# A two-product attention-MLP kernel: the first product from scaled f16 pairs instead of float32r, its straddling tiles as two 64-column halves

## The chip, the cores and the metric

The kernel runs on one core of one Trainium2 chip. The metric is device time in microseconds (us) of one execution. The names of the engines are those of the profile: PE is TensorE (PEld its weight loads), DVE is VectorE, ACT is ScalarE, POOL is GpSimd, SP is SyncE, which issues the DMAs.

## The reference

Eight batches of eight heads, 576 positions of 64 numbers. Thirty-two "pack" queries p attend to k and v; the result serves as keys and values for q. The attention output, as rows of 512 numbers, goes through an MLP of width 1024 with a softmax gate and a layer norm:

```python
p_packed = sm_attn(p, k, v)
x = sm_attn(q, p_packed, p_packed)      # rows of 8 heads x 64 = 512
h = x @ w_in                            # 4608 x 1024
e = np.exp(h - h.max(-1))
solu = h * e / (e.sum(-1) + 1e-9)
ln = (solu - solu.mean()) / np.sqrt(solu.var() + 1e-6) * g_ln
out = ln @ w_out                        # 4608 x 512
```

w_in and w_out come as 64-bit floats, which the kernel reads as two 32-bit words each; it builds f32 values of w_in and a high and a low f16 part of w_out from them. The other inputs are f32.

## The kernel before, in words

The work of a batch b has three parts. `pack(b)` transposes k (kT, L350), takes the scores of p (L368) in two PSUM banks of the pool ps_a, their exponentials (L381), transposes these (L397), multiplies with v (L407), scales the result to pp (L411), transposes it on PE (L413) and copies it to ppT on DVE (L415). `unpack(b)` transposes q (L428), takes the scores of q against ppT (16 small matmuls, L467), transposes them on DVE (L439), does the softmax (maximum L443, subtraction on POOL L444, exponential on ACT L446, sum L448, reciprocal, product on POOL L451), and computes z = ppT . w_in (L483), so that the first product can be written h = a2 . z with the softmax weights a2 as left side. Both are split into a high and a low part: z into zh (a rounding cast on ACT, L485) and zl (a subtraction on DVE, L500), a2 after a transpose (L505) into a2h (ACT, L507) and a2l (DVE, L508).

The rows of the output are cut in 36 tiles of 128. For each, `mlp_in` sums in the bank pair h (pool ps_h, two buffers) three products, a2h.zh, a2h.zl and a2l.zh, for two head groups r and two column halves n: 12 matmuls 128x512 in float32r (L521). 576 is four and a half tiles, so every second tile border straddles two batches: four such tiles, each with rows of an even batch b and of b+1. There the tiles a2h and a2l have 64 zero columns of padding, and 24 full matmuls are summed. Then come the row maximum nm (DVE, L523), a bound of two small operations (L525, L526), its reciprocal s_row (L528), the exponential e with bias nm (ACT, L531), and u = e.s_row.h (DVE, L534). `mlp_norm` subtracts the mean (POOL L542) into an f16 pair yhl (ACT L544, DVE L545), which a transposing DMA on SP's queue turns into yT (L547); the squares and a row factor c_row go over ACT and POOL. `mlp_out` makes 24 f16 matmuls 128x512 (L564) in a bank of ps_o, DVE scales them to o_sb (L566), and SP stores (L571).

What sets the order: the program is written tile by tile, with tables (`FIRST_BATCH`, `LATER`, `LOADS`, `PACK0` and so on) that say how many steps of pack and unpack are taken ahead of, in and behind each tile, and with priorities. From batch 1 on PE's order is as written, by the tables; the other engines, and PE in batch 0, are ordered by a scheduler that simulates the program. pack runs two batches ahead of the tiles, unpack one. At the start, batch 0, w_in, w_out and the first pack are prepared (`high_part`, `add_low_part`, `prepare_w_out`), and PE runs filler matmuls (`keep_busy`).

## Time and profile before

| | us |
|---|---|
| median of 3 runs | 472.3 |
| lowest and highest run | 471.37 and 472.42 |
| span of the profiled execution | 468.9 |
| PE busy | 430.2 (92%) |
| DVE busy | 354.2 (76%) |
| ACT busy | 232.4 (50%) |
| POOL busy | 148.0 (32%) |

The runs are 3.4 us above the span in the median, which is what lies around the profiled part. A line of the profile's groups names the kernel line, the engine, the operation and its tile names, the number of instructions, then busy time, mean time of one in ns, and the engine's idle time before them with what ended it. The chain of waits is the work that ended last, followed back from the end; each of its pieces has a start, a length and a line. A row by stretch of time gives the length, the busy time of PE, PEld, DVE, ACT and POOL, the granted clock of PE, the share of the DMA engines and GB/s.

### The profile page before, as it was taken

Reading aid. Unit: us, or ns where it says so; the run is one execution under the profiler, and the core shown is the slowest. Engines: PE = TensorE matmul, PEld = TensorE weight load, DVE = VectorE, ACT = ScalarE, POOL = GpSimd, SP = SyncE. Lnnn points to the kernel's source line nnn. Section 1 sums busy time; section 2 is a strip of 40 time slices with the busy share of each in tenths; the row PEclk is TensorE's granted clock in tenths of the full one; section 3 lists DMA queues with packets and bytes.
Section 4 is the critical chain, followed back from the end, with each engine's and each line's share of the span. In section 5 each row is a group of like instructions: output and inputs, shape, how many; then the busy total and the mean of one; then the engine's idle time right before and its main releaser. Section 6 shows DMA issues by size and latency. Waiting matters only on the chain.

```text
span 468.9 us, 8271 instructions
## 1 busy us (share of the span) xinstructions
PE 430.2 (92%) x3116; PEld 234.7 (50%) x3116; DVE 354.2 (76%) x648; ACT 232.4 (50%) x404; POOL 148.0 (32%) x244
## 2 busy tenths in 40 slices
PE   9697795859979999999899998999999999999995
PEld 7472244633434555446544554566445555575552
DVE  3568989778768887988489979975898688655551
ACT  3577848654343653565244562653356536433430
POOL 3424556935103211421044123311342142111220
PEclk9979759988998999999999999999999999999999
DMA  9999999999569969965989588339035333526342
GB/s 265 336 268 286 152 207 124 135 193 155 110 138 185 169 127 181 191 142 95 204 111 135 109 177 154 89 69 214 23 68 113 69 69 83 119 67 134 70 101 78
DMA packets 237880, 67.00 MB, mean 143 GB/s; under 512 B 208912, under 2 KB 231440, under 8 KB 237328
## 3 DMA queue, kind: packets, MB, share of 16 engines
q1 hardware_dynamic: 237840, 66.48, 74.3%
q8 instruction: 24, 0.39, 0.4%
q14 instruction: 16, 0.13, 0.1%
HBM read 37.23 MB, written 9.44 MB: 100 GB/s over the span
## 4 chain that ended last, share of the span: by engine, by line
PE 58%; DVE 18%; DMA 10%; POOL 5%; issue 4%; SPq 2%; ACT 2%; DVEq 0%; ACTq 0%; POOLq 0%
PE po L564 30%; PE h L521 17%; DMA yT<-yhl 4%; DMA zh<-in_moe_w_in_dram 3%; PE pa L483 3%; PE pa L407 2%; PE pa L368 2%; DMA v_sb<-in_v_dram 2%; PE pa L397 2%; DVE yhl L545 2%; DVE nm L523 2%; DVE kT L350 2%; DVE u L534 1%; DMA p2raw<-in_p_dram 1%; PE pa L467 1%
## 5 line engine op out<-in xcount | busy, mean ns | idle before, releaser
L564 PE MATMUL po<-wch,yT 128*128 128x512 f16 x576 | 178.6, 380 | 4.5 <-DMA yT<-yhl 4.5
L564 PEld LDWEIGHTS <-yT 128*128 128x128 f16 x864 | 81.0, 98 | 116.5 <-issue 17.5
L564 PE MATMUL po<-wcl,yT 128*128 128x512 f16 x288 | 108.8, 379 | 0.0
L531 ACT ACTIVATE e<-h,nm 128x1024 f32<-128x1024 f32 x36 | 40.0, 1112 | 69.5 <-DVE nm L523 69.5
L521 PE MATMUL h<-zh,a2h 128*128 128x512 f32 x160 | 69.9, 437 | 1.7 <-DVE u L534 1.7
L544 ACT ACTIVATE yhl<-u,negmu 128x1024 f16<-128x1024 f32 x36 | 41.4, 1149 | 53.1 <-POOL negmu L542 51.2
L521 PE MATMUL h<-zl,a2h 128*128 128x512 f32 x160 | 64.2, 401 | 0.6 <-POOL zl L493 0.6
L521 PE MATMUL h<-zh,a2l 128*128 128x512 f32 x160 | 64.7, 404 | 0.0
L545 DVE SCALAR_TENSOR_TENSOR yhl<-u,negmu,yhl 128x1024 f16<-128x1024 f32 x36 | 48.5, 1346 | 15.5 <-ACT yhl L544 15.5
L523 DVE TENSOR_REDUCE nm<-h 128x1 f32<-128x1024 f32 x36 | 43.9, 1219 | 20.6 <-PE h L521 20.5
L534 DVE SCALAR_TENSOR_TENSOR u<-e,s_row,h 128x1024 f32<-128x1024 f32 x36 | 45.8, 1271 | 7.1 <-ACT e L531 5.0
L551 POOL TENSOR_SCALAR s_eps<-se,s_row 128x1 f32<-128x1 f32 x36 | 10.8, 301 | 110.9 <-ACT e L531 56.0
L554 POOL TENSOR_SCALAR c_row<-sq,s_eps 128x1 f32<-128x1 f32 x36 | 18.8, 521 | 78.9 <-ACT e L549 78.9
L549 ACT ACTIVATE e<-u,negmu 128x1024 f32<-128x1024 f32 x36 | 40.9, 1136 | 3.4 <-POOL negmu L542 3.4
L566 DVE SCALAR_TENSOR_TENSOR o_sb<-po,c_row,inv 128x512 f32<-128x512 f32 x36 | 26.7, 743 | 20.9 <-PE po L564 20.8
L521 PEld LDWEIGHTS h<-zh,a2h 128*128 128x128 f32 x160 | 31.2, 195 | 17.4 <-issue 8.2
L521 PEld LDWEIGHTS h<-zh,a2l 128*128 128x128 f32 x160 | 30.9, 193 | 8.7 <-DVE a2l L508 1.2
L521 PEld LDWEIGHTS h<-zl,a2h 128*128 128x128 f32 x160 | 31.0, 194 | 7.1 <-POOL zl L493 0.9
L485 ACT CAST zh<-pa 128x512 fp32r<-128x512 f32 x28 | 15.1, 583 | 23.3 <-PE pa L483 23.3
L444 POOL TENSOR_TENSOR s<-s,mx 128x576 f32<-128x576 f32 x14 | 16.9, 1229 | 30.2 <-DVE mx L443 30.1
L381 ACT ACTIVATE e<-pa,nmx 128x288 f32<-128x288 f32 x28 | 13.8, 499 | 21.6 <-DVE nmx L373 21.6
L221 POOL TENSOR_TENSOR u<-u 128x1024 fp32r<-128x1024 f32 (+1 forms) x5 | 12.9, 2573 | 28.3 <-ACT u L220 18.1
(138 smaller groups left out, 608.5 us busy)
## 6 DMA issues: line engine op xcount, KB each, us to landing
out_dram<-o_sb SPq DMA_DIRECT2D x36, 256.0 KB, 2.3
v_sb<-in_v_dram SPq DMA_DIRECT2D x16, 512.0 KB, 6.0
raw<-in_k_dram SPq DMA_DIRECT2D x28, 288.0 KB, 6.3
raw<-in_q_dram SPq DMA_DIRECT2D x96, 72.0 KB, 2.6
zh<-in_moe_w_in_dram SPq DMA_DIRECT2D x2, 1024.0 KB, 7.0
zl<-in_moe_w_in_dram SPq DMA_DIRECT2D x2, 1024.0 KB, 8.6
raw<-in_q_dram SPq DMA_DIRECT2D x4, 512.0 KB, 9.3
raw<-in_moe_w_out_dram SPq DMA_DIRECT2D x2, 1024.0 KB, 5.9
```

What stands on the lines that cost most here:

```text
L444: eng.tensor_tensor(out=s2[r], in0=s2[r], in1=mx.unsqueeze(2).broadcast_to([P, NB, J]), op=ALU.subtract)
L485: nc.scalar.copy(z_h[:, r, cols], pz)
L521: nc.tensor.matmul(h[:, 512 * n:512 * n + 512], lhsT=lhsT, rhs=z[:, r, 512 * n:512 * n + 512], start=t == 0, stop=t == len(terms) - 1)
L523: nc.vector.tensor_reduce(out=nm, in_=h, axis=AX.X, op=ALU.max, negate=True)
L531: nc.scalar.activation(e, h, AF.Exp, bias=nm, accum_out=se)
L534: nc.vector.scalar_tensor_tensor(out=u, in0=e, scalar=s_row, in1=h, op0=ALU.mult, op1=ALU.mult, accum_out=su)
L544: nc.scalar.activation(yhl[:, 0], u, AF.Identity, bias=negmu)
L545: nc.vector.scalar_tensor_tensor(out=yhl[:, 1], in0=u, scalar=negmu, in1=yhl[:, 0], op0=ALU.add, op1=ALU.subtract)
L549: nc.scalar.activation(e, u, AF.Square, bias=negmu, accum_out=sq)
L554: nc.gpsimd.tensor_scalar(out=c_row, in0=sq, scalar1=1.0 / DF, scalar2=s_eps, op0=ALU.mult, op1=ALU.add)
L564: nc.tensor.matmul(po, lhsT=yT[:, a, c], rhs=w[:, c], start=c == 0 and t == 0, stop=c == NFC - 1 and t == 2)
L566: nc.vector.scalar_tensor_tensor(out=o_sb, in0=po, scalar=c_row, in1=inv, op0=ALU.mult, op1=ALU.mult)
```

## The change

The four operands zh, zl, a2h and a2l become f16, each scaled by a power of two so that it fits; the straddling tile becomes 12 pairs of matmuls with 64 columns each, one half of a pair for each batch, into PSUM partitions 0 to 63 and 64 to 127. The zero padding and the four POOL operations that wrote it are gone.

The scale comes from a bound: at the start, eight f32 matmuls of ones with the absolute high words of w_in (L212) and a maximum give w_bound; in each batch a peak of |pp| (DVE, L425) and a 128x1 matmul that sums it (PE, L426, into a spare column of the bank that holds pp's transpose) give a power of two in three small DVE operations (L436 to L438) and three on POOL (L439 to L441). The factors stand in the tile unit. zh is an activation with that factor, zl a scalar_tensor_tensor. In each row tile the exponential gets a bias of its own (L551, one more small DVE operation between nm and the exponential). In a straddling tile POOL copies unit from the two batches (L536).

In the changed kernel the lines are shifted: L540 is L521, L585 is L564, L502 is L483, L486 is L467, L421 is L413, L423 is L415, L542 is L523, L544, L545 and L547 are L525, L526 and L528, L555 is L534, L510 is L500, L517 is L508, L566 is L545, L587 is L566.

```diff
+        if chunk < G:
+            for i in range(2):
+                nc.tensor.matmul(w_sums[0], lhsT=ones_f, rhs=bits.bitcast(F32)[:, 512 * i:512 * i + 512], start=chunk + i == 0, stop=chunk == G - 1 and i == 1)
+            if chunk == G - 1:
+                nc.vector.tensor_reduce(out=w_bound, in_=w_sums[0], axis=AX.X, op=ALU.max)
...
-        a2h.append(par.tile([P, 2, S + LEFT], F32R, name=f'a2h{par_i}'))
-        a2l.append(par.tile([P, 2, S + LEFT], F32R, name=f'a2l{par_i}'))
-        pad = slice(S, S + LEFT) if par_i == 0 else slice(0, LEFT)
-        for t in (a2h[-1], a2l[-1]):
-            nc.gpsimd.tensor_scalar(out=t[:, :, pad], in0=ones_f.rearrange('p (r x) -> p r x', r=2), scalar1=0.0, scalar2=None, op0=ALU.mult)
+        a2h.append(par.tile([P, 2, S], F16, name=f'a2h{par_i}'))
+        a2l.append(par.tile([P, 2, S], F16, name=f'a2l{par_i}'))
...
-        packed[b] = ppT
+        peak = small.tile([P, 1], F32, name='peak')
+        nc.vector.tensor_reduce(out=peak, in_=pp.rearrange('p r d -> p (r d)'), axis=AX.X, op=ALU.max, apply_absolute_value=True)
+        nc.tensor.matmul(ppt[:, P:P + 1], lhsT=ones_f, rhs=peak, start=True, stop=True)
+        packed[b] = (ppT, ppt)
...
+        nc.vector.tensor_scalar(out=power, in0=ppt[:, P:P + 1], scalar1=w_bound, scalar2=2.0 ** (-40), op0=ALU.mult, op1=ALU.max)
+        nc.vector.tensor_scalar(out=power.bitcast(I32), in0=power.bitcast(I32), scalar1=2139095040, scalar2=None, op0=ALU.bitwise_and)
+        nc.vector.tensor_scalar(out=unit[:, 0:1].bitcast(I32), in0=power.bitcast(I32), scalar1=-1, scalar2=254 + Z_TOP << 23, op0=ALU.mult, op1=ALU.add)
...
+                nc.scalar.activation(z_h[:, r, cols], pz, AF.Copy, scale=unit[:, 0:1])
...
+                    nc.vector.scalar_tensor_tensor(out=z_l[:, r, cols], in0=pz, scalar=unit[:, 0:1], in1=z_h[:, r, cols], op0=ALU.mult, op1=ALU.subtract)
...
-        for i, c in parts:
-            cols = slice(c, c + P)
+        m = P // len(parts)
+        groups = []
+        for x, (i, c) in enumerate(parts):
+            rows, cols = (slice(m * x, m * x + m), slice(c, c + m))
...
+            for t, side_by_side in enumerate(zip(*groups)):
+                for rows, lhsT, z, r in side_by_side:
+                    nc.tensor.matmul(h[rows, 512 * n:512 * n + 512], lhsT=lhsT, rhs=z[:, r, 512 * n:512 * n + 512], start=t == 0, stop=t == last)
...
-        nc.scalar.activation(e, h, AF.Exp, bias=nm, accum_out=se)
+        bias = small.tile([P, 1], F32, name='bias')
+        nc.vector.tensor_scalar_mul(bias, nm, unit[:, 1:2])
+        nc.scalar.activation(e, h, AF.Exp, bias=bias, scale=unit[:, 1:2], accum_out=se)
```

Three places in the order of the instructions matter below. The first is PE behind the transpose of pp in pack 6 (at 320 us of the profile before); pa is the bank of the transpose, po the output product. Before:

```order
L564 MATMUL po<-wch,yT 128x512
L413 MATMUL pa<-ident,pp 128x128
L564 LDWEIGHTS yT
L564 MATMUL po<-wch,yT 128x512
L564 MATMUL po<-wcl,yT 128x512
```

The same place after; qT and ppT are the operands of the q scores:

```order
L585 MATMUL po<-wch,yT 128x512
L421 MATMUL pa<-ident,pp 128x128
L486 MATMUL pa<-qT,ppT 32x288
L426 MATMUL pa<-peak,ones_f 128x1
L585 LDWEIGHTS yT
L585 MATMUL po<-wch,yT 128x512
```

One of the 16 q scores and the peak matmul moved between the transpose and the 12 output matmuls that followed it; the other 15 scores stay behind these. The same stands at packs 3 to 7.

The second is PE in the straddling tile of batches 4 and 5; a2h_182 and a2h_186 are the parities of the two batches. Before:

```order
L521 MATMUL h<-zh,a2h_182 128x512
L521 MATMUL h<-zl,a2h_182 128x512
L521 MATMUL h<-zh,a2l_183 128x512
L521 MATMUL h<-zh,a2h_186 128x512
L521 MATMUL h<-zl,a2h_186 128x512
L521 MATMUL h<-zh,a2l_187 128x512
```

After, a2h_183 and a2h_185 are the two batches:

```order
L540 LDWEIGHTS a2h_183
L540 MATMUL h<-zh,a2h_183 64x512
L540 LDWEIGHTS a2h_185
L540 MATMUL h<-zh,a2h_185 64x512
L540 LDWEIGHTS a2h_183
L540 MATMUL h<-zl,a2h_183 64x512
L540 LDWEIGHTS a2h_185
L540 MATMUL h<-zl,a2h_185 64x512
```

The two batches take turns, matmul by matmul, each with 64 columns and a weight load of its own.

The third is DVE around the second tile of batch 3 (at 254 us before); a2l, yhl, mx (a maximum of pack scores) and nmx belong to other tiles than nm. Before:

```order
L545 SCALAR_TENSOR_TENSOR yhl<-u,negmu,yhl 128x1024
L508 TENSOR_TENSOR a2l_183<-s_2927,a2h_182 128x576
L523 TENSOR_REDUCE nm<-h 128x1
L371 TENSOR_REDUCE mx_2667<-pa 128x1 x2
L525 TENSOR_SCALAR bound<-nm 128x1
L373 TENSOR_REDUCE nmx<-mx_2667 128x1
L526 TENSOR_SCALAR bound<-nm,bound 128x1
L528 RECIPROCAL s_row<-bound 128x1
L534 SCALAR_TENSOR_TENSOR u,su<-e,s_row,h 128x1024
```

After:

```order
L542 TENSOR_REDUCE nm<-h 128x1
L566 SCALAR_TENSOR_TENSOR yhl<-u,negmu,yhl 128x1024
L379 TENSOR_REDUCE mx_2767<-pa 128x1 x2
L544 TENSOR_SCALAR bound<-nm,unit 128x1
L517 TENSOR_TENSOR a2l_184<-s_3031,a2h_183 128x576
L551 TENSOR_SCALAR bias<-nm,unit 128x1
L381 TENSOR_REDUCE nmx<-mx_2767 128x1
L545 TENSOR_SCALAR bound<-nm,bound 128x1
L547 RECIPROCAL s_row<-bound 128x1
L555 SCALAR_TENSOR_TENSOR u,su<-e,s_row,h 128x1024
```

yhl and one a2l moved from ahead of nm to between nm and the new bias.

More of the change, by code (lines that the diff above doesn't have):

```diff
@@ L257, in packed_attention_solu_kernel @@
     nc.scalar.activation(warm, ones_f[:, :1], AF.Exp)
+    w_bound = const.tile([P, 1], F32, name='w_bound')
     neg_half = const.tile([P, 1], F32, name='neg_half')
@@ L505, in unpack @@
             nc.vector.transpose(out=a2T, in_=a2[r].rearrange('p a j -> p (a j)'))
[L506 removed]
+            hi, lo = (a2h[b % 2][:, r], a2l[b % 2][:, r])
             nc.scalar.copy(hi, a2T)
[L508 removed]
+            (nc.vector if b else EN(nc, A2L_BY[r])).tensor_tensor(out=lo, in0=a2T, in1=hi, op=ALU.subtract)
             yield
```

65 lines of the change are left out of this document (33 added, 32 removed).

## The prediction

> **What bounds the kernel now.** I read the page first: the span and the chain that ended last.
>
> ```profile
> span 468.9 us, 8271 instructions
> PE 58%; DVE 18%; DMA 10%; POOL 5%; issue 4%; SPq 2%; ACT 2%; DVEq 0%; ACTq 0%; POOLq 0%
> PE po L564 30%; PE h L521 17%; DMA yT<-yhl 4%; DMA zh<-in_moe_w_in_dram 3%; PE pa L483 3%; PE pa L407 2%; PE pa L368 2%; DMA v_sb<-in_v_dram 2%; PE pa L397 2%; DVE yhl L545 2%; DVE nm L523 2%; DVE kT L350 2%; DVE u L534 1%; DMA p2raw<-in_p_dram 1%; PE pa L467 1%
> ```
>
> PE is 58% of the chain, not all of it. So a PE saving counts only where PE ends last. The chain of waits in order of time gives the places.
>
> ```profile
> 144.48 3.49 PE h L521 x12
> 180.77 5.34 DMA v_sb<-in_v_dram
> 227.38 6.81 DMA yT<-yhl
> 280.52 7.02 DMA yT<-yhl
> 323.33 2.06 PE h L521 x9
> 326.04 3.64 PE h L521 x15
> 371.72 2.60 PE po L564 x12
> 402.91 2.74 PE h L521 x12
> 405.66 5.20 PE po L564 x24
> 410.85 8.18 PE h L521 x36
> 445.29 2.74 PE h L521 x12
> ```
>
> From 144.48 to 445.29 the chain holds 22 full tiles of first product (x12). I count 21: one, at 270, lies between a stretch on DVE and one on DMA. Two straddling tiles stand on it too: 24 instructions at 323.33 and 326.04, and 24 of the 36 at 410.85. The straddling tile at 226 ends in a wait for a DMA (227.38). The one before 126 belongs to the startup. The busy times by stretch tell where DVE is the bound:
>
> ```profile
> 186.00:203.00 17.00, 16.20 (x97) 8.22 (x96) 16.13 (x33) 8.79 (x15) 6.55 (x9) 1.00 1.19 179
> 237.00:268.00 31.00, 31.00 (x188) 15.45 (x186) 29.95 (x56) 15.86 (x28) 11.07 (x17) 1.00 0.78 115
> 288.00:329.00 41.00, 41.00 (x308) 23.28 (x307) 31.70 (x65) 20.76 (x37) 10.09 (x23) 1.00 0.51 116
> ```
>
> The columns are PE, PEld, DVE, ACT, POOL, clock. In 186 to 203 DVE works 16.13 of 17 us, in 237 to 268 29.95 of 31, and the chain runs on it; in 288 to 329 it has 9 us to spare and the chain is PE's.
>
> **The change, part by part.**
>
> *The matmul's type.* At 402.91 twelve matmuls take 2.74 us, 228 ns each. The f16 ones behind them (24 in 5.20) take 217 ns. If f16 brings the first product to the same rate, an ordinary tile saves 12 x 11 = 0.14 us; 21 tiles, 2.9 us. The low end is no saving, if the 11 ns belong to the accumulation and not to the type.
>
> *The straddling tile.* Before: 24 x 228 ns = 5.47 us. After: 24 half-width matmuls, two of which may run side by side: 12 x 217 = 2.60, so -2.87. That two 64-column halves share the array is shown by another pair of rows, both f32 with 128 columns streamed: 16 halves take as long as 8 full ones, whose row stands second.
>
> ```profile
> 13.62 1.09 PE L125 MATMUL h<-ident,raw 128*64 128x128 f32 x16
> 215.45 0.95 PE pa L397 x8
> ```
>
> I take -2.87; the other end is 24 x 217 = 5.21, -0.26. The difference is 2.6 us a tile. On the chain: 2 x 2.87 = 5.7.
>
> The page "TensorE: Matmul & The Clock Gate" of the Trainium skill, Part 3, says that a weight load overlaps matmuls in flight only where the row group differs. Two column halves have the same row group, so by that rule the halves need not overlap and the saving would be -0.26. The rows above are f32 without separate weight loads, so no run here shows it; the case is a rival below.
>
> *The straddling tile at 226.* Its next PE work waits for a transposing DMA that stands on SP's queue behind q and v loads:
>
> ```profile
> 217.59 6.23 SPq L85 DMA_DIRECT2D raw<-in_q_dram  x9
> 227.38 3.47 SPq L547 DMA_TRANSPOSE yT<-yhl  x1
> 232.40 0.39 PE L521 MATMUL h<-zh,a2l 128*128 128x512 f32 x1
> 234.23 0.39 PE L564 MATMUL po<-wch,yT 128*128 128x512 f16 x1 [1.44 <-DMA yT<-yhl]
> ```
>
> The order on SP is the same after the change here. So 2.87 us off PE only lengthens the wait of 1.44. Counted at nothing.
>
> *The peak matmul and a score ahead of it.* In the new order PE takes one q score matmul, which needs the copy of ppT, directly behind the transpose of pp. Before, twelve output matmuls stood there:
>
> ```profile
> 320.46 0.27 PE L413 MATMUL pa<-ident,pp 128*128 128x128 f32 x1
> 320.57 0.38 PE L564 MATMUL po<-wch,yT 128*128 128x512 f16 x1
> 320.77 0.29 DVE L415 COPY ppT<-pa 128x128 f32<-128x128 f32 x1 [0.90 <-PE pa L413]
> 325.32 0.72 PE L467 MATMUL pa<-qT,ppT 64*32 64x288 f32 x16
> ```
>
> PE would idle from 320.57 until the copy has ended (321.06), then run the lone score and the peak matmul before it resumes: 0.5 + 0.3 + 0.05 = 0.85 us. Behind it are the 12 output matmuls and all else of PE. It happens five times (packs 3 to 7). At 181, 224 and 277 a DMA wait follows and takes it up; at 320 and 371 the chain is PE's: +1.7. Both ends: 0.9 if the copy is earlier, 3 if DVE has queued something ahead of it.
>
> *VectorE.* Rows for the new operations:
>
> ```profile
> L566 DVE SCALAR_TENSOR_TENSOR o_sb<-po,c_row,inv 128x512 f32<-128x512 f32 x36 | 26.7, 743 | 20.9 <-PE po L564 20.8
> L500 DVE TENSOR_TENSOR zl<-pa,zh 128x512 fp32r<-128x512 f32 x28 | 18.0, 678 | 0.0
> L525 DVE TENSOR_SCALAR bound<-nm 128x1 f32<-128x1 f32 x36 | 5.1, 143 | 0.5
> ```
>
> A batch adds 4 x (743 - 678) = 0.26 us for zl, 4.5 biases and 3 power-of-two steps at 0.14 (1.1), and a peak reduction of 128x128, like the copy of ppT (0.29, above): 1.6 us. Beside spare DVE time this is free. In 237 to 268 it is on the path, with one thing more. The exponential, which used to follow nm at once, now waits for the bias:
>
> ```profile
> 256.54 1.22 DVE L523 TENSOR_REDUCE nm<-h 128x1 f32<-128x1024 f32 x1
> 257.79 1.11 ACT L531 ACTIVATE e<-h,nm 128x1024 f32<-128x1024 f32 x1 [2.48 <-DVE nm L523]
> 259.10 0.93 DVE u L534
> ```
>
> In the new order yhl, two reductions and an a2l stand between this nm and its bias, so e starts about 2.7 us later, and after the bias only three smalls (0.4) cover its 1.11 before u: DVE waits about 0.9. So +2.3 in batch 3, where that happens once (1.6 less 0.2 for parts outside, plus 0.9), and +1.0 in the other DVE stretch (186 to 203), where fewer of the operations fall: +3.3 together. Ends: 1.0 (smalls hidden in the gaps between long operations) and 6.
>
> *POOL, ACT.* The scale pointers change no shape. The units and their copies on POOL (three per batch, two per straddling tile) are taken from idle time there (11.07 busy of 31). Nothing, unless units for a straddling tile come after nm: 0.3.
>
> *Startup.* New: eight f32 matmuls for w_bound. PE pays 0.5 each (two in 1.02), on an engine that runs filler matmuls then. Other things move: SP issues 16 q loads, not 11, ahead of the first yT.
>
> ```profile
> 34.65 1.02 PE L226 MATMUL pa<-w_in_sb,ident 128*128 128x512 f32 x2
> 88.79 7.99 SPq L85 DMA_DIRECT2D raw<-in_q_dram  x11
> 99.38 4.77 SPq L547 DMA_TRANSPOSE yT<-yhl  x1
> 108.24 0.39 PE L564 MATMUL po<-wch,yT 128*128 128x512 f16 x1
> ```
>
> Five loads at 0.73 put that yT at 103.0, its end at 107.8 and the first output matmul about where it was (108.2); but scores and z matmuls that were done before 108 now come behind it, up to +3. Against that, the shorter straddling tile (-2.87) ahead of the chain that ran to 144.48. The sum is +1, my estimate, from -3 to +5.
>
> **Sum.** -2.9 - 5.7 + 1.7 + 3.3 + 1.0 = -2.6 us. The times shown are 3.4 us above the span, 472.3 against 468.9, so 466.3 + 3.4 = 469.7.
>
> **Rivals.**
>
> *The startup loses (slower).* The tables that order the startup are unchanged while the work they order is not. For it: five more loads before yT, and ppT's copy behind other DVE work. Against: the last piece of that chain, through POOL, comes out alike. If the end of the startup moves by more than 1 + 2.6 = 3.6 us, the kernel is slower; I price it at +6, so -2.9 - 5.7 + 1.7 + 3.3 + 6 = +2.4: 474.7.
>
> *The halves run one after the other.* Each straddling tile on the chain loses 2.6: -2.6 + 5.2 = +2.6, and 474.9. For it: each half now has its own weight load, which no row before has with 64 columns. Against: the pair of rows above.
>
> *PE's clock falls at 231.* The wait at 234.23 grows from 1.44 to 1.44 + 2.87 - 0.85 = 3.5 us. The trace has one such case, in the startup:
>
> ```profile
> 101.77 1.55 PE L467 MATMUL pa<-qT,ppT 64*32 64x288 f32 x16 [4.71 <-DVE s L439]
> 104.16 0.63 PE L521 MATMUL h<-zl,a2h 128*128 128x512 f32 x1
> 102.00:106.00 4.00, 3.75 (x22) 2.02 (x14) 3.95 (x11) 1.87 (x4) 1.46 (x5) 0.50 1.36 195
> ```
>
> After 4.71 us idle the clock was 0.50 for 4 us, and matmuls came 0.43 us apart, not 0.23; after the 1.44 it stood at 1.00 (237 to 268). 3.5 lies between. A fall costs PE about 3 us, of which the stretch on DVE behind hides about 1: 469.7 + 2 = 471.7, no change. The clock gate's section in the same page of the Trainium skill (Part 1) puts the drop at an idle window of about 3.4 us; by that it would happen here in about half the executions. The trace agrees with both its sides.
>
> *Everything counts.* The startup keeps its straddling tile's 2.87 and more (-3) and DVE's smalls are hidden (1.0): -2.9 - 5.7 + 1.7 + 1.0 - 3.0 = -8.9, 463.4.
>
> **How the numbers follow.** Chances: forecast 0.42 (faster 0.35, same 0.05, slower 0.02), startup 0.20 (slower 0.18, same 0.02), halves one by one 0.13 (slower 0.12, same 0.01), clock 0.13 (faster 0.04, same 0.05, slower 0.04), everything 0.12 (faster). That is faster 0.51, same 0.13, slower 0.36, with 0.2% (0.9 us) as what a measurement can tell. The range must take the rivals of both signs and reach beyond 463.4 and 474.9 by the bounds of DVE and startup: 462 to 479. The forecast's own range is 466.5 to 472.5.
>
> **What would show it.** Right: groups of the first product with 64-column matmuls whose starts come in pairs 0.22 us apart; full tiles of 2.60 us; straddling tiles of 2.6 to 2.7; a PE gap of about 0.5 behind each pp transpose with the ppT copy as releaser; a DVE idle before u for e in batch 3; first output matmul near 108 and the chain's batch-1 work from about 145. Wrong: straddling tiles over 4 us (halves in turn); clock under 0.9 behind 234; a first tile of batch 1 later than 148, in which case my sum falls in the startup; or DVE-bound stretches longer by more than 3 us each.

## The result and the profile after

| | before | after |
|---|---|---|
| median of four runs, us | 471.94 | 490.95 |
| lowest and highest run | 471.37 and 472.42 | 489.56 and 493.89 |
| span of the profiled execution | 468.9 | 487.8 |

The ratio is 1.0423, with an interval from 1.0382 to 1.0463: slower by 19.0 us in the medians and 18.9 in the span. The head of the page and its chain, after:

```profile
span 487.8 us, 8442 instructions
PE 42%; DVE 31%; DMA 9%; issue 6%; SPq 5%; ACT 4%; POOL 3%; DVEq 0%; ACTq 0%; POOLq 0%
PE po L585 21%; PE h L540 9%; DMA yT<-yhl 4%; DVE nm L542 3%; SPq L87 3%; DVE yhl L566 3%; DMA zh<-in_moe_w_in_dram 3%; DVE qT L447 2%; PE pa L486 2%; DMA v_sb<-in_v_dram 2%; DVE zl L510 2%; PE pa L415 2%; DVE mx L379 2%; DVE kT L358 2%; PE pa L405 2%
PEclk9989789878975899999999999999999999999999
```

The clock row before, in slices of 11.7 us:

```profile
PEclk9979759988998999999999999999999999999999
```

PE's share of the chain fell from 58% to 42%, and DVE's rose from 18% to 31%. The last row after is the clock in 40 slices of 12.2 us: below 9 it stands only in the first 14 slices, that is in the first 170 us. Before, it is below 9 in the first 13 slices too, so the clock row alone does not place the loss. The starts of the row maximum nm do: there is one in each of the 36 row tiles, it has the same meaning in both kernels, and it can be read off DVE's part of the timeline.

| nm of | before, us | after, difference | of that, new since the row above |
|---|---|---|---|
| first tile of batch 0 | 71.42 | +12.27 | +12.27 |
| third tile of batch 0 | 94.87 | +1.96 | -10.31 |
| straddling tile of batches 0 and 1 | 125.73 | +12.08 | +10.12 |
| first tile of batch 1 | 150.03 | +16.42 | +4.34 |
| straddling tile of batches 2 and 3 | 232.83 | +17.61 | +1.19 |
| first tile of batch 3 | 246.33 | +20.09 | +2.48 |
| last tile | 448.07 | +18.75 | -1.34 |

The startup, which here means the time up to the first tile of batch 1, lost 16.4 us, and everything behind it 2.3. The first loss of 12 us, in the first tile, is nearly recovered by the third; the one that stays arises between 95 and 166 us. Four stretches of it, after; the columns are the length, the busy time of PE, PEld, DVE, ACT and POOL, the clock, the DMA share and GB/s:

```profile
109.00:113.00 4.00, 3.68 (x9) 1.34 (x10) 2.46 (x3) 3.46 (x5) 1.04 (x5) 0.50 0.42 92
126.00:138.00 12.00, 11.16 (x89) 3.41 (x86) 10.13 (x19) 4.81 (x10) 2.31 (x2) 1.00 1.31 182
138.00:150.00 12.00, 5.25 (x82) 3.33 (x78) 8.06 (x19) 5.89 (x13) 1.61 (x5) 0.64 0.35 57
150.00:166.00 16.00, 13.38 (x109) 4.83 (x102) 10.18 (x23) 2.63 (x4) 3.16 (x6) 0.63 0.98 173
```

Before, the same place:

```profile
108.00:126.00 18.00, 18.00 (x104) 8.04 (x97) 13.63 (x25) 7.97 (x16) 6.70 (x7) 1.00 0.93 131
126.00:150.00 24.00, 20.28 (x206) 9.82 (x205) 18.66 (x40) 8.45 (x16) 3.89 (x8) 0.93 0.74 145
```

Before, PE was busy for 38.3 of these 42 us, at a clock of 1.00 and 0.93. After, it is busy for 5.25 of 12 us from 138 on, and works at 0.64 and 0.63 for 28 us. From the third nm of batch 0 to the first of batch 1, summed over stretches of 1 us, PE's time has three parts: idle time, busy time multiplied by what the clock lacked of 1.00, and busy time multiplied by the clock, which is called work here.

| | length | idle | lost to the clock | work |
|---|---|---|---|---|
| before | 55.2 | 8.7 | 4.6 | 41.8 |
| after | 69.6 | 17.1 | 11.0 | 41.5 |

In this stretch PE has the same work to do; it waits 8.4 us more and loses 6.4 more to the clock. From the start of the program on the balance is another: 27.6 us idle, 17.5 lost to the clock and 104.9 of work before; 37.1, 18.2 and 111.2 after. Ahead of the third nm the changed kernel does 6.6 us more work and loses 5.5 less to the clock; its eight new matmuls for w_bound (L212) are busy there for 9.5 us. What PE waits for behind the third nm, after, by the view of waits from 95 to 167 us (us in total, times, longest):

```profile
PE pa L405 <- ACT e L389: 4.7, 1, 4.7
PE h L540 <- DVE u L555: 4.3, 1, 4.3
PE po L585 <- DMA yT<-yhl: 2.2, 1, 2.2
PE pa L415 <- ACT e1T L406: 2.0, 1, 2.0
PE pa L486 <- DVE ppT L423: 1.8, 2, 1.4
```

The longest one belongs to pack 2's own chain: scores, exponential, transposes of e (L405), product with v (L415). PE stands still for each of its steps. On the other engines at that place, after:

```profile
137.71 1.07 PE L376 MATMUL pa<-kT,pT 64*32 64x288 f32 x16
137.81 1.23 DVE L542 TENSOR_REDUCE nm<-h 128x1 f32<-128x1024 f32 x1 [0.95 <-PE h L540]
139.75 1.43 DVE L358 STREAM_TRANSPOSE kT<-raw 128x576 f32<-128x576 f32 x2
141.19 0.20 DVE L551 TENSOR_SCALAR bias<-nm,unit 128x1 f32<-128x1 f32 x1
141.51 1.20 ACT L552 ACTIVATE e<-h,bias,unit 128x1024 f32<-128x1024 f32 x1 [3.48 <-DVE bias L551]
142.87 0.50 ACT L389 ACTIVATE e<-pa,nmx 128x288 f32<-128x288 f32 x1
143.51 0.97 PE L405 MATMUL pa<-ident,e 128*128 128x128 f32 x2 [4.74 <-ACT e L389]
```

The new bias stands behind the maxima of pack 2's scores and a transpose on DVE, the tile's exponential starts on ACT after 3.48 us of idling for it, and the exponential of pack 2 stands behind that one on ACT; PE has nothing else. It had before, which the order of PE shows. Batch 0's part of it follows, from the transpose of pack 1's pp on, with the program's instructions counted; in the traces an f32 matmul that is not a transpose shows as two records. T stands for that transpose; S: q scores of batch 1; z; po: output matmuls of batch 0; h: straddling tile; k: scores of pack 2; e: its transposes; av: its product with v; pk: peak.

```
before: T1 h12 S16 h6 z8 po22 z4 po1 z4 po15 h2 po5 h2 k4 h1 k4 h13 po12 k8 po17 e10 av40 T1 S16 z8 h12
after:  T1 S4 pk1 po20 h1 po2 S8 po19 S2 z3 S1 z1 S1 po22 z4 po9 z4 h6 z4 k4 h4 k4 h13 k8 e10 av40 T1 S1 pk1 S15 z8 h12
```

Before, 29 of batch 0's 72 output matmuls stood between the scores of pack 2 and its transposes, as cover for the exponential. After, all 72 stand ahead of them, and none is left. The change touched no table; the scheduler that simulates batch 0 set this order for the changed instructions.

### The profile page after: what moved, and what is told of

The parts are those of the page before. It is cut to its first block, busy times and chain, and to the rows that moved or that the text cites. A ratio compares the mean times of both kernels' runs of the same rounds, so it can differ in the third digit from the quotient of the medians.

```text
span 487.8 us, 8442 instructions
## 1 busy us (share of the span) xinstructions
PE 432.9 (89%) x3148; PEld 192.3 (39%) x3148; DVE 368.8 (76%) x717; ACT 238.7 (49%) x404; POOL 153.5 (31%) x272
## 4 chain that ended last, share of the span: by engine, by line
PE 42%; DVE 31%; DMA 9%; issue 6%; SPq 5%; ACT 4%; POOL 3%; DVEq 0%; ACTq 0%; POOLq 0%
PE po L585 21%; PE h L540 9%; DMA yT<-yhl 4%; DVE nm L542 3%; SPq L87 3%; DVE yhl L566 3%; DMA zh<-in_moe_w_in_dram 3%; DVE qT L447 2%; PE pa L486 2%; DMA v_sb<-in_v_dram 2%; DVE zl L510 2%; PE pa L415 2%; DVE mx L379 2%; DVE kT L358 2%; PE pa L405 2%
## 5 line engine op out<-in xcount | busy, mean ns | idle before, releaser
L585 PE MATMUL po<-wch,yT 128*128 128x512 f16 x576 | 180.8, 383 | 6.0 <-DMA yT<-yhl 6.0
L585 PEld LDWEIGHTS <-yT 128*128 128x128 f16 x864 | 82.4, 99 | 118.0 <-issue 16.3
L585 PE MATMUL po<-wcl,yT 128*128 128x512 f16 x288 | 110.0, 383 | 0.0
L552 ACT ACTIVATE e<-h,bias,unit 128x1024 f32<-128x1024 f32 x36 | 43.3, 1203 | 66.3 <-DVE bias L551 53.6
L540 PE MATMUL h<-zh,a2h 128*128 128x512 f16 (+1 forms) x160 | 58.8, 391 | 5.4 <-DVE u L555 4.3
L540 PE MATMUL h<-zh,a2l 128*128 128x512 f16 (+1 forms) x160 | 57.9, 388 | 1.4 <-DVE a2l L517 1.4
L540 PE MATMUL h<-zl,a2h 128*128 128x512 f16 (+1 forms) x160 | 57.9, 389 | 1.2 <-POOL zl L508 1.1
L555 DVE SCALAR_TENSOR_TENSOR u<-e,s_row,h 128x1024 f32<-128x1024 f32 x36 | 45.7, 1268 | 17.3 <-ACT e L552 16.2
L566 DVE SCALAR_TENSOR_TENSOR yhl<-u,negmu,yhl 128x1024 f16<-128x1024 f32 x36 | 46.9, 1304 | 15.1 <-ACT yhl L565 15.1
L542 DVE TENSOR_REDUCE nm<-h 128x1 f32<-128x1024 f32 x36 | 43.8, 1216 | 11.0 <-PE h L540 10.6
L540 PEld LDWEIGHTS <-a2h 128*128 128x128 f16 (+1 forms) x320 | 28.8, 102 | 46.4 <-issue 14.3
L587 DVE SCALAR_TENSOR_TENSOR o_sb<-po,c_row,inv 128x512 f32<-128x512 f32 x36 | 26.6, 739 | 19.1 <-PE po L585 18.9
L504 ACT ACTIVATE zh<-pa,unit 128x512 f16<-128x512 f32 x28 | 17.9, 682 | 38.4 <-PE pa L502 38.4
L465 ACT ACTIVATE a<-s 128x576 f32<-128x576 f32 x16 | 10.9, 683 | 32.2 <-POOL s L463 26.0
L576 POOL TENSOR_TENSOR c_row<-c_row,neg_half 128x1 f32<-128x1 f32 x36 | 24.5, 682 | 3.0
L486 PE MATMUL pa<-qT,ppT 64*32 64x288 f32 x224 | 18.9, 453 | 6.5 <-DVE ppT L423 3.7
L458 DVE STREAM_TRANSPOSE s<-pa 128x288 f32<-128x288 f32 x28 | 11.9, 460 | 15.8 <-PE pa L486 15.8
```

The costliest lines, as they stand in the source:

```text
L486: nc.tensor.matmul(out_, lhsT=lhsT, rhs=rhs, start=True, stop=True)
L540: nc.tensor.matmul(h[rows, 512 * n:512 * n + 512], lhsT=lhsT, rhs=z[:, r, 512 * n:512 * n + 512], start=t == 0, stop=t == last)
L542: nc.vector.tensor_reduce(out=nm, in_=h, axis=AX.X, op=ALU.max, negate=True)
L552: nc.scalar.activation(e, h, AF.Exp, bias=bias, scale=unit[:, 1:2], accum_out=se)
L555: nc.vector.scalar_tensor_tensor(out=u, in0=e, scalar=s_row, in1=h, op0=ALU.mult, op1=ALU.mult, accum_out=su)
L566: nc.vector.scalar_tensor_tensor(out=yhl[:, 1], in0=u, scalar=negmu, in1=yhl[:, 0], op0=ALU.add, op1=ALU.subtract)
```

## The experiments

After the result there were three candidates for the startup: the work that the factors added, the new type and halves themselves, and the order. The first four kernels separate the parts of the change.

**Parts alone.** e1_f16_padded is the kernel before with f16 for the four operands, without factors, and still padded. e2_f16_halves adds the 64-column halves. Both leave out the factors.

```diff
-        a2h.append(par.tile([P, 2, S + LEFT], F32R, name=f'a2h{par_i}'))
+        a2h.append(par.tile([P, 2, S + LEFT], F16, name=f'a2h{par_i}'))
...
-        for i, c in parts:
+        for x, (i, c) in enumerate(parts):
+            rows, cols = (slice(m * x, m * x + m), slice(c, c + m))
```

> The kernel before with the four operands in f16 and nothing else: no scaling factors (z and a2 are only rounded, so small low parts lose digits), zero padding and 24 full matmuls in the straddling tile. Its order of DMAs at the start is that of the kernel before. Theory A (the loss is the reordered startup and a little of DVE's new work per batch; f16 itself gains): the startup's end, read at the first row maximum of batch 1, stays at 150 us within 1; 21 tiles of 0.14 us and two straddling tiles of 24 x 11 ns on the chain give about 3.4 us less, 468.5. Rival B (f16 itself slows something: the product, or the casts on ACT and DVE): no gain or a loss, 472 to 480, with tiles of 2.7 us or more.

> The same with the straddling tile as 12 pairs of 64-column halves without padding, still without scaling factors (none of w_bound, peak, units and bias). Theory A: the halves run side by side and nothing of the startup moves to later: two straddling tiles at 2.6 us less on the chain, so about 5 us less than the padded one, 463.5. Rival B (halves in turn): 468 to 469, straddling tiles of about 5.2 us. Rival C (the straddling tile's saving is waited away elsewhere): the tile takes 2.6 us and the time stays at 468.

e1 467.49 us, ratio 0.9922 (0.9891 to 0.9953); e2 465.91, 0.9893 (0.9856 to 0.9929), beside 471.49. Type and halves together are a gain; the 1.6 us between the two medians are less than the spread of either kernel's runs (2.7 and 2.5). In e2 the first tile of batch 1 is 1.6 us earlier than before, not 16 later, and PE's order in batch 0 is before's in the main: batch 1's scores stand ahead of the output matmuls, and 27 of the output matmuls stand between the scores of pack 2 and its transposes. That clears type and halves of the startup's loss.

e3_const_scale is the changed kernel with factors that are constants: the bound of w_in, peak, power and the units are left out; the bias, the scaled casts and zl stay. e4_no_wsum keeps all but the eight matmuls and the maximum for w_bound, and takes 4.0 for that.

```diff
-        unit = units[row // S]
+        unit = unit_c
```

> The changed kernel with a constant power of two in place of the measured one: w_bound, the peak, its matmul, the power and unit operations and their copies are left out; the activation with a factor, the scalar_tensor_tensor for zl, the bias and the exponential with a scale stay. So this is the f16 halves plus bias and factors. Theory A: the startup is reordered in part (14 q loads ahead of the first transposing DMA, not 16): first row maximum of batch 1 at 152 to 160; behind it about 1.5 us more than the f16 halves in the DVE stretches; 466 to 476. Rival D (all of the loss is in the peak and unit operations): 464 to 465.

> The changed kernel with w_bound set to a constant: the eight f32 matmuls and the reduction at the start are left out, all operations per batch stay. Theory A: the startup is reordered less (12 q loads ahead of the first transposing DMA): first row maximum of batch 1 at 152 to 162 and not 166.5; what lies behind it as in the changed kernel (321.3 us from there to the end); 476 to 486. Rival E (the eight matmuls cost nothing, the loss at the start is from the peak and its wait): 490 within 2.

e3 485.75, 1.0302 (1.0255 to 1.0349); e4 486.83, 1.0327 (1.03 to 1.0355). With the whole chain that makes the factors left out (e3), 14.3 of the 19 us remain, and 15.3 without w_bound alone (e4); the first tile of batch 1 stands at +13.6 and +9.2. In e3 PE has 98.5 us of work up to there, less than before's 104.9, with 37.2 idle and 27.9 lost to the clock. So the amount of added work is not the main cause. What w_bound adds lies early: the first nm is at 82.6 to 85.6 us in the five kernels of this case that have it, and at 69.7 to 75.9 in the others; e4's third nm is 7.3 us earlier than the changed kernel's, and from there to the first tile of batch 1 both take about 69.7.

**The place of the q scores: a theory that fell.** I then took it that the loss came from batch 1's q scores, which now stand behind output matmuls that wait for yT (T1 S4 ... po20 above). One number of a table sets the first batch's priority; raised, it brings them earlier. e5_const_early is e3 with it, e6_after_early and e7_after_earliest are the changed kernel with two values.

```diff
-FIRST_BATCH = [..., [1000, 375], [0, -400, -50], 190]
+FIRST_BATCH = [..., [1000, 375], [0, -400, -50], 1000]
```

> The kernel with a constant scale (e3: no w_bound, peak, power, unit operations) with one number of the table for batch 0 changed: the priority offset of pack 1, 190 to 1000. In its order all 16 q scores of batch 1 and twelve h matmuls stand ahead of the first output matmuls on PE, as in the kernel before, where e3 has 22 output matmuls ahead of them; and 9 q loads stand ahead of the first transposing DMA, not 14. Theory A (the order of the startup costs what it costs, not the new operations themselves): first row maximum of batch 1 at 147 to 152 and not 163.7; 485.8 less 13 = 470 to 474. Rival F (the new operations cost the time wherever the order puts them): 480 or more.

> The changed kernel itself with the same one number changed (190 to 1000). On PE 12 of the 16 q scores of batch 1 now stand ahead of the first output matmuls, where the changed kernel has 4; SP's order stays (16 q loads ahead of the first transposing DMA). Theory A: the part of the startup's loss that comes from the scores behind the output matmuls goes: first row maximum of batch 1 at 156 to 161 and not 166.5; 481 to 486. Rival F: 489 to 492.

> The same with 3000: the same 12 scores in one piece ahead of the output matmuls, but the peak matmul ahead of all of them, so that all scores wait for the peak. Theory A: within 2 us of the kernel with 1000. If the peak's wait is what costs in the startup: later by 3 or more.

e5 483.92 (1.0203 to 1.0299), e6 492.13 (1.0411 to 1.0459), e7 493.56 with 3000 (1.0424 to 1.0528). None brings the startup back; e5 has it at +13.4, e6 at +14.8, e7 at +17.5. The place of these scores alone is not the cause.

**One small operation on DVE.** e8_halves_bias is e2 with a bias that multiplies nm by 1.0 on DVE and for which the exponential waits: no factor, only the wait.

```diff
-        nc.scalar.activation(e, h, AF.Exp, bias=nm, accum_out=se)
+        bias = small.tile([P, 1], F32, name='bias')
+        nc.vector.tensor_scalar_mul(bias, nm, 1.0)
+        nc.scalar.activation(e, h, AF.Exp, bias=bias, accum_out=se)
```

> The f16 halves without factors (e2, 465.9) with one thing added: the small DVE operation that makes a bias from nm (here times 1), on which the exponential waits. In its order the 16 scores of batch 1 stay ahead of the output matmuls; 15 q loads, not 11, stand ahead of the first transposing DMAs. If the bias is what costs in the DVE stretches (my 0.14 each and 0.9 where u waits for e): from the first row maximum of batch 1 to the end 2 to 4 us more than in e2; together with a startup within 3 us of e2's: 468 to 472. If the bias is free: 465 to 467. If the order of the startup is what the four more q loads make it: first row maximum of batch 1 at 153 or later, 472 to 476.

479.18, ratio 1.0154 (1.0135 to 1.0172): 13.3 us above e2, for 36 operations of 0.14 us. In the profiled executions, where the last tile is 15.8 us later, the startup takes 10.2 (first tile of batch 1 at +8.7, in e2 at -1.6), and the rest 5.5: behind the startup e2 gains 4.5 on the kernel before, and e8 loses 1.0. The startup in e8:

```profile
138.00:150.00 12.00, 8.54 (x123) 4.63 (x123) 2.90 (x11) 2.51 (x7) 0.00 (x0) 0.55 0.80 146
```

A clock of 0.55, and DVE busy for 2.90 of 12 us: there the wait is not DVE's work. From the third nm to the first tile of batch 1, PE waits once for the exponential of pack 2, 5.2 us (e2 1.4), and once for the first yT, 4.3 (e2 0.5). Of the 5.5 behind the startup, 3.0 arise in batch 3 and 1.4 in batch 5. Batch 5 of the changed kernel shows how, on DVE:

```profile
371.50 1.22 DVE L542 TENSOR_REDUCE nm<-h 128x1 f32<-128x1024 f32 x1
372.64 1.27 DVE L566 SCALAR_TENSOR_TENSOR yhl<-u,negmu,yhl 128x1024 f16<-128x1024 f32 x1
375.35 0.21 DVE L551 TENSOR_SCALAR bias<-nm,unit 128x1 f32<-128x1 f32 x1
376.98 1.28 DVE L555 SCALAR_TENSOR_TENSOR u<-e,s_row,h 128x1024 f32<-128x1024 f32 x1 [1.04 <-ACT e L552]
```

DVE reaches the bias 3.85 us after nm began and then waits 1.04 for the exponential that it released itself so late. This is the wait that the prediction had for one tile of batch 3. In e8 it is 0.85 to 0.95 us in two tiles of batch 3 and three of batch 5.

**The same bias on ACT.** e11_bias_act is e8 with the bias as an operation of ACT, so that nothing of DVE's queue stands between.

```diff
-        nc.vector.tensor_scalar_mul(bias, nm, 1.0)
+        nc.scalar.mul(bias, nm, 1.0)
```

> e8 (f16 halves and a bias operation, 479.2) with the bias made by ACT, directly ahead of the exponential, and not by DVE. In e8 the kernel loses 5.5 us against e2 behind the startup, in batches 3 and 5, where DVE's order puts long operations between nm and the bias and then waits for e. If that wait is the cost: behind the first row maximum of batch 1, 0.5 to 2.5 us more than e2 and not 5.5. If ACT's extra operation costs as much (two more handings over per tile): 5 or more. The startup keeps an order of its own (16 q loads ahead of the first transposing DMA): 470 to 478 in all.

471.19, ratio 0.9999 (0.9973 to 1.0026). Behind the startup it gains 5.1 us, as e2 does (4.5): the 5.5 are gone. DVE's wait in the third tile of batch 5, 0.95 in e8:

```profile
363.68 1.28 DVE L530 SCALAR_TENSOR_TENSOR u<-e,s_row,h 128x1024 f32<-128x1024 f32 x1 [0.27 <-ACT e L527]
```

The startup keeps +3.3. e12_const_act, which is e5 with that move, came to 477.52 (ratio 1.005 to 1.0154), first tile of batch 1 at +6.7 where e5 had +13.4. Its runs lie between 473.67 and 481.38, and the profiled one is the lowest.

> The constant scale (e3, 485.8) with the bias on ACT and the number of e5 (pack 1 at 1000). Its order at the start is the nearest to that of the kernel before: all 16 scores of batch 1 ahead of the output matmuls, 10 q loads ahead of the first transposing DMAs, and 20 output matmuls between the straddling tile and pack 2's transposes. Theory A refined: PE's idle and slow time between the third row maximum and batch 1's first is 12 to 18 us, not 33; first row maximum of batch 1 at 149 to 154; 465 to 472, so not slower than the kernel before. If factors and the scalar_tensor_tensor cost in themselves: over 476.

**Filling pack 2's gap: a miss.** If PE lost its cover there, that is, work to do while it waits, work put into the gap should keep the clock up. e9_fill is the changed kernel with 9 matmuls behind pack 2's scores and 4 behind its transposes, into a bank that nobody reads.

```diff
+            if r == 1:
+                filler(b, kT[:, 0, :512], 9)
...
+        filler(b, e1[:, 1, :512], 4)
```

> The changed kernel with 13 f32 filler matmuls (results unused) in pack 2, nine that read kT and four that read e1, in a bank of the output product. The order that comes of it has four of them and 24 output matmuls among the transposes and products of pack 2, where the changed kernel has PE idle. Theory A, refined by e5 to e8 (the startup loses by PE waiting, 17 us against 9 between the third row maximum and the first of batch 1, and by the clock that falls with it, 11 us against 5, not by work): first row maximum of batch 1 at 158 to 163 and not 166.5, with a clock over 0.8 from 138 to 158; 482 to 488. Rival G (a chain of dependences as long whatever PE does meanwhile): 490 to 494.

497.75, 1.0549 (1.0512 to 1.0587), 6.8 above the changed kernel. The nine did not come into the gap. They need nothing but kT, and PE took them some 60 us ahead of it; only the four that read e1 stand in the gap (each matmul is two records):

```profile
79.44 7.99 PE L354 MATMUL po<-kT,ident 128*128 128x512 f32 x18 [0.40 <-DVE kT L364]
147.79 5.25 PE L354 MATMUL po<-e,ident 128*128 128x512 f32 x8
```

The third nm is 6.2 us later than in the changed kernel, which is most of the loss. From there to the first tile of batch 1 it takes 70.6 us for 69.6: idle time fell from 17.1 to 13.9 us and the clock's loss from 11.0 to 9.8, but the work rose from 41.5 to 46.8. So these four cost about what they covered, and filling the whole gap was not tested.

**The straddling tile of batches 2 and 3.** In e2 the first tile of batch 3 stands at +1.5, after -3.9 at the straddling tile ahead of it: 5.4 us given back within 13. PE there, in e2:

```profile
233.34 0.39 PE L558 MATMUL po<-wch,yT 128*128 128x512 f16 x1 [4.41 <-DMA yT<-yhl]
236.84 0.85 PE L466 MATMUL pa<-qT,ppT 64*32 64x288 f32 x2
232.00:236.00 4.00, 2.66 (x8) 1.04 (x9) 0.76 (x2) 2.28 (x3) 0.54 (x3) 0.73 1.11 252
236.00:240.00 4.00, 4.00 (x27) 1.07 (x26) 1.05 (x3) 0.00 (x0) 0.64 (x2) 0.84 0.00 0
```

The wait for yT, 1.44 us before, is 4.41, the clock is down in both stretches behind it, and batch 3's q scores stand behind nine of the output matmuls that waited, with DVE idle for want of them. e10_halves_fill puts 13 f16 matmuls into that gap, e14_halves_fill8 only 8.

```diff
+        if row == 2 * S + S - LEFT:
+            idle = ps_o.tile([P, DM], F32, name='po')
+            for _ in range(13):
+                nc.tensor.matmul(idle, lhsT=a2h[0][:, 0, :P], rhs=zh[0][:, 0, :512], start=True, stop=True)
```

> The f16 halves without factors (e2, 465.9) with 13 filler matmuls (128x512 f16, results unused) behind the straddling tile of batches 2 and 3, where the halves save 2.9 us and PE then waits for a transposing DMA; in e2 the clock was 0.73 and 0.84 in the 8 us behind and 5.4 us were given back by the next row maximum. If the idle time lowers the clock there: clock 1.00 from 232 to 240, first row maximum of batch 3 three to four us earlier against the straddling tile's, 461 to 463.5. If it is the DMA's lateness or the order of the scores alone: 465 to 467.

> e2 with eight filler matmuls (1.7 us, results unused) behind the straddling tile of batches 2 and 3 and not 13. In its order one output matmul, which waits for the transposing DMA, still stands ahead of the q scores, where e10 has only fillers ahead of them; PE's wait for the DMA becomes 2.7 us and not 4.4. If the clock is what costs in e2: clock 1.00 from 232 to 240, and from the straddling tile's row maximum to batch 3's first 15 to 16.5 us (e2 18.9, e10 13.2); 461.5 to 464. If only the place of the scores helps: as e2, 18 or more, 465 to 467.

e10 459.48, ratio 0.9742 (0.9716 to 0.9768); e14 462.04, 0.98 (0.9785 to 0.9814). The same stretch in e10:

```profile
229.92 0.67 PE L466 MATMUL pa<-qT,ppT 64*32 64x288 f32 x2
232.00:236.00 4.00, 4.00 (x20) 1.85 (x19) 4.00 (x8) 2.28 (x3) 0.86 (x3) 1.00 0.73 137
```

And in e14:

```profile
232.05 0.39 PE L558 MATMUL po<-wch,yT 128*128 128x512 f16 x1 [2.65 <-DMA yT<-yhl]
232.00:236.00 4.00, 3.95 (x22) 1.00 (x23) 0.97 (x3) 2.28 (x3) 0.81 (x2) 0.65 0.74 141
```

In e10 the clock stays at 1.00 and the scores go in at 229.92, seven us earlier than in e2, ahead of the output matmuls, so that DVE is busy for 4.00 of 4 us. e14 fills half the gap; its scores go in from 232.37 on, 4.5 us earlier than in e2, but the clock still falls, to 0.65 in the mean of these 4 us. From the straddling tile's nm to the next, e2 takes 18.9 us, e14 17.2 and e10 13.2. So the scores' earlier start, with the clock still falling, brought 1.6 of 5.6, which lies between the two outcomes that the expectation names. In the medians e10 gains 6.4 us on e2, e14 3.9. In e10 the scores go in among the fillers, DVE gets its work sooner, and the clock stays up. e10 is faster than both kernels, by 11.6 us than before beside it (471.1) and by 31 than the changed one, but it has no factors.

**Bias and fillers together.** e13_after_mended is the changed kernel with the bias on ACT and the 13 fillers; e15_const_mended is e12 with the fillers.

```diff
-        nc.vector.tensor_scalar_mul(bias, nm, unit[:, 1:2])
+        nc.scalar.activation(bias, nm, AF.Copy, scale=unit[:, 1:2])
```

> The changed kernel with the bias on ACT and 13 filler matmuls behind the straddling tile of batches 2 and 3 (results unused); its order at the start keeps what the changed kernel has there, 4 scores of batch 1 ahead of the output matmuls and 16 q loads ahead of the first transposing DMA. If my accounting holds (startup 16.4 of the 18.9 us of span lost; behind it bias 5.5 and the wait 2.5, against gains of the product): first row maximum of batch 1 still at 164 to 168, from there to the end 7 to 9 us less than in the changed kernel, 481 to 485. If the startup is not a cost of its own: 475 or less.

> e12 (constant factors, bias on ACT, pack 1 at 1000; 477.5) with the 13 fillers of e10. From the straddling tile's row maximum to batch 3's first e12 took 18.7 us; with fillers 13 to 14.5, so 472 to 474 by the median of e12, with a startup as in e12.

e13 484.28, 1.0275 (1.0259 to 1.029): 6.7 us better in the median and 4.4 in the profiled executions, all of it behind the startup, whose end stays at +16.5. e15 469.97, 0.9962 (0.9942 to 0.9982): with constant factors, the bias on ACT, the fillers and e5's number the change is a gain of 0.4%, with the first tile of batch 1 still at +7.6.

**The order alone.** The last two kernels are e2 with other numbers in a table of batch 0's priorities: the same operations, in another order.

```diff
-PACK0 = [-350, 400, 2010, 365, -1000, 60, -2800, 200, 200]
+PACK0 = [-350, 400, 2010, 365, -1000, 60, 0, 200, 200]
```

That is e16_order_only. e17_order_scores has, in e2's table UNPACK0, 0 and 0 for 1965 and 1025.

> e2 (f16 halves, 465.9, no scaling factors) with one number of the table for pack 0 changed (-2800 to 0), no operation added or left out. Its order at the start becomes like that of the changed kernel and of e3: 8 of the 16 scores of batch 1 behind 19 output matmuls and the z products behind 26 more, only the last ones ahead of pack 2's transposes left to cover them, none between; 15 q loads ahead of the first transposing DMA. If the order alone loses the time: first row maximum of batch 1 at 158 to 166 (e2 148.5), PE idle and slow 24 us or more before it; 475 to 483. If the new operations are needed for the loss: 148 to 153, 465 to 470.

> e2 with two numbers of the table for unpack 0 changed (1965, 1025 to 0, 0): all 16 scores of batch 1 stay ahead of the output matmuls and 17 output matmuls stay between the straddling tile and pack 2's transposes, as in e2; but 16 q loads stand ahead of the first transposing DMAs, not 11. If the q loads are what delays: first row maximum of batch 1 at 152 to 157; 469 to 474. If the scores' place is what matters and the loads are not: within 1.5 us of e2, 464.5 to 467.5.

e16 479.23, ratio 1.0159 (1.012 to 1.0197), 13.3 us above e2; e17 472.04, 1.0026 (0.999 to 1.0062), 6.1 above. The first tile of batch 1 moves by 9.1 and 6.3 us. In e16 it looks like the changed kernel:

```profile
128.00:138.00 10.00, 4.94 (x49) 1.32 (x45) 7.58 (x17) 4.45 (x9) 0.81 (x4) 0.78 0.25 78
138.00:160.00 22.00, 17.47 (x182) 7.51 (x183) 14.76 (x32) 6.18 (x14) 5.12 (x6) 0.71 0.89 151
```

PE idle for half of 10 us, then a clock of 0.71. Over the same stretch as in the table above, e16 has 17.6 us of idle time and 8.4 lost to the clock, e2 9.8 and 7.1. So an order of batch 0 alone, with no operation added, costs 9.1 us in the startup, more than half of the 16.4.

e17 shows a second way. All 16 scores stay ahead of the output matmuls, and pack 2 keeps its cover: 17 output matmuls ahead of its last scores and 15 ahead of its transposes. But 16 q loads, not 11, stand on SP's queue ahead of the first yT, which is issued at 103.25 where e2 has 100.36. PE's wait for it (us in total, times, longest) is, in e17 and then in e2:

```profile
PE po L558 <- DMA yT<-yhl: 6.4, 1, 6.4
PE po L558 <- DMA yT<-yhl: 0.5, 1, 0.5
```

The expectation for the loads as the cause (first tile of batch 1 at 152 to 157; 469 to 474) is what came: 154.8 and 472.04. The changed kernel has these 16 loads too, with a wait of 2.2 us.

## Why the prediction was wrong

The forecast was 469.7, and the median is 490.95: 21.3 off. Of that 15.4 lie in the startup's term and 5.9 behind it.

*The matmul's type: right.* Full tiles take 2.59 us for 2.74, 0.15 each where 0.14 was forecast:

```profile
408.45 2.59 PE h L540 x12
432.89 5.41 PE h L540 x36
```

*The straddling tiles: right, at the one where nothing else interferes.* The second row answers to 8.18 us before, a straddling tile and a full one: 2.77 us less on the chain, for a forecast of 2.87 and 0.14. By the starts of the matmuls, from the tile's first to the next product's, it is 5.31 for 8.38. The halves go in pairs, in the rows of the straddling tile of batches 4 and 5:

```profile
346.48 0.38 PE L540 MATMUL h<-zl,a2h 128*64 128x512 f16 x2
346.70 0.38 PE L540 MATMUL h<-zh,a2l 128*64 128x512 f16 x2
```

Two matmuls every 0.22 us. The rival of halves in turn is refuted. With it falls, for this form, the rule from Part 3 of "TensorE: Matmul & The Clock Gate" in the Trainium skill, that a weight load overlaps a matmul in flight only where the row group differs. Each half has a weight load of its own in the same rows, and the pair keeps the pace of one full matmul. What the same part says of loads into a background weight buffer is not touched by this. The traces of the kernel before could have told it. The prediction says that its f32 rows are without separate weight loads, but they have them, 16 with 64 columns beside the 16 halves; and each full matmul of the first product, at 228 ns, had one of 128 columns that took 0.19 us within that time:

```profile
13.61 0.85 PEld L125 LDWEIGHTS h<-ident,raw 128*64 128x64 f32 x16
```

*The startup: the step that failed.* The prediction put it at +1, from -3 to +5, as a sum of the work that moved: five more loads ahead of yT, against a shorter straddling tile. Its loads were right: yT was issued at 102.67, forecast 103.0, and the first output matmul stood at 109.32 for about 108. Its 0.5 us for each of the eight w_bound matmuls was not: the row with two in 1.02 us is one f32 matmul as two records, and the eight are busy for 9.5 us, not 4. But the term took the rest of the order as before's. What the runs showed: the simulated scheduler set another order of batch 0 for the changed operations; it puts all output matmuls ahead of pack 2's chain; PE has nothing to cover it, idles 8.4 us more behind the third nm, and its clock falls, for 6.4 us more. The rival for it had the right sign and +6 as its price; it was the right mechanism in its first sentence (tables unchanged, work changed), and its price took loads and queues and not cover and clock. Loads can cost by themselves (6.3 us at that tile in e17), but here yT came as forecast. The prediction named its own test, a first tile of batch 1 later than 148; that tile's nm, at 150.03 before, starts at 166.45.

What is shown of this cause, and what isn't: that behind the third nm the work is the same and the loss is idle time and clock (the two traces); that neither type nor halves cost it (e2); that one small operation brings 10 us of loss there (e8) and a table number without any operation 9 (e16). Not shown is that the whole 16.4 is order. No kernel here has all the factors and before's order in batch 0. With constant factors and a bias on ACT 6.7 stay (e12), and what the chain of w_bound and units takes by itself was not separated: e4 has 7.2 us less at that tile than the changed kernel, all of it ahead of the third nm, but the same first-batch scheduler reacts to that edit too. The work hides one thing more: by the same sum e2 has 36.6 us of it in this stretch, so the halves' saving does not show in the changed kernel's 41.5.

*DVE: mechanism right, too small.* It was put at 3.3, with one wait for e in batch 3. e8 against e2 gives 5.5 for the bias alone: 3.0 in batch 3, where 2.3 was forecast, 1.4 in batch 5, for which there was nothing, and 0.9 ahead of batch 3, for 1.0. In the changed kernel other waits cover part of it: e13 ends 4.4 us better than the changed kernel behind the startup, 2.2 of it at the straddling tile of batches 2 and 3, so about 2.2 for the bias.

*The lone score and the peak matmul: too small.* 0.85 each was forecast, two on the chain. Pack 6, after:

```profile
342.06 0.27 PE L421 MATMUL pa<-ident,pp 128*128 128x128 f32 x1
342.72 0.67 PE L486 MATMUL pa<-qT,ppT 64*32 64x288 f32 x2 [0.38 <-DVE ppT L423]
343.32 0.38 PE L426 MATMUL pa<-peak,ones_f 128*128 128x1 f32 x2
343.56 0.38 PE L585 MATMUL po<-wch,yT 128*128 128x512 f16 x1
```

From the transpose to the next output matmul it is 1.50 us, and 0.11 before: 1.4 each. Of it 0.66 go by until the scores begin (the transpose, and 0.38 of waiting for the copy), 0.60 until the peak, where 0.3 was forecast, and 0.24 until the output matmul, where it was 0.05. In a row of 16 records (0.72 us before) a score, which is two records, takes 0.09. Five such places are 7 us at most. e13 loses 5.95 us more than e15 behind the startup, and these two differ by w_bound, peak, power, units and one number of batch 0's table. The loss comes in five steps of 1.2 to 1.4 us, at the first tiles of batches 2, 4 and 6 and at the straddling tiles of batches 2 and 3 and of 4 and 5, one for each of packs 3 to 7. So all five count, where the prediction let DMA waits take up three. No run removes the peak matmul alone, so its price stays an estimate.

*The straddling tile at 226, counted at nothing.* In the profiled execution of the changed kernel this was nearly right: the wait grew from 1.44 to 2.19 us, forecast 3.5, and the clock stayed at 1.00; 1.2 us are gained and 2.5 given back. The wait, and the stretch that begins with it:

```profile
252.59 0.39 PE L585 MATMUL po<-wch,yT 128*128 128x512 f16 x1 [2.19 <-DMA yT<-yhl]
252.00:256.00 4.00, 3.41 (x15) 1.32 (x15) 1.61 (x5) 2.24 (x3) 0.79 (x3) 1.00 0.84 191
```

The rival of the falling clock did not come there, but that was luck. In e4, e6 and e7, whose edits lie in the startup, the same wait was 3.19, 2.69 and 2.45 us and the clock fell to 0.50 for 3.4 us behind it. It fell in e2 too, where 5.4 are given back. Part 1 of the same page of the Trainium skill puts the drop at an idle window of about 3.4 us. The 4.41 of e2 agrees with that; the 2.65 of e14, with 0.65 behind it, and the three of e4, e6 and e7 came below that figure.

The sum behind the startup, by the runs: the product's gain of 8.74 (e10 from the first tile of batch 1 to the last), less 0.68 for constant factors (e15), 5.95 for what makes them (e13 against e15), 2.22 for the straddling wait and 2.22 for the bias: a loss of 2.33, where the prediction had a gain of 3.6. Each term is the difference of two profiled executions, so the sum must come out; and a fall of the clock that comes in one execution and not in another moves such a difference by some us. e4 takes 5.1 us more behind the startup than the changed kernel, with the same operations there.

## What to carry to other kernels

Where a scheduler's simulation sets an order, the price of an edit there is not the sum of its operations: compare the whole order of the startup, and count what PE can do during each wait, and which loads stand ahead of it, before costing anything. A small operation between a reduction and its consumer may be better off on the consumer's engine: here long operations of other tiles stood ahead of it on DVE, and with it on ACT the 5.5 us behind the startup were gone (e11). PE saved ahead of a DMA wait lengthens that wait, and can cost the clock and with it more than was saved, as in e2; what helped in e10 was to bring work that others wait for ahead of the waiting instruction.
